# First loads and warm-up of a two-branch attention kernel: one weight quarter behind a small activation, warm-up matmuls on a constant

## Chip, cores and metric

The kernel runs on one core of one Trainium2 chip. The metric is the device time of one execution in microseconds, so smaller is better. Each figure is a median of several runs unless it is called a profile, which is one execution.

## The reference

```python
x = A_x                                             # (1, 2048, 1024), bf16
g = sigmoid((x * gate_w).sum(-1, keepdims=True))
a = _A_ref(x, A_wqkv, A_wo)                         # linear attention, 32 heads of 32
b = _B_ref(x, B_wqkv, B_wo)                         # dilated local window of 8 keys
return g * a + (1 - g) * b

def _A_ref(x, wqkv, wo):
    q, k, v = split(x @ wqkv)                       # cut: reshape to heads
    phi = lambda t: where(t > 0, t + 1, exp(t)) + 1e-6
    # cut: kv = phi(k)^T v, num = phi(q) kv, den = phi(q) . sum(phi(k)), o = num / den
    return o @ wo
```

Only the beginning matters here: the first work on TensorE is `x @ wqkv` for the keys of branch A. It needs x transposed and the key weights.

## The kernel before

The kernel loads x transposed (`xT`) and the key weights (`WkA`, two halves of 512 columns) in slices of the contraction dimension. A slice `k` holds two blocks of 128 rows; its 128x2x512 piece of one half is called a quarter here, because a half has four of them. The first quarters (k=0) of both halves go out on ScalarE's DMA queue. All other loads go out on SyncE's.

```python
nc.scalar.preload_act_table_set("natural_log_exp_and_others")
# ... cut ...
load_wk(nc.scalar, 0, 0)          # first half, first quarter
load_wk(nc.scalar, 0, 1)          # second half, first quarter
with tc.manual_schedule(engines={SP}):
    load_xT(0, 0, 2)              # "the first transpose": 256 rows of x, slice 0
    load_xT(0, 2, 4)              # "the second transpose"
    for k in range(1, 4):
        load_wk(nc.sync, k, 0)
        load_xT(k, 0, 4)
        load_wk(nc.sync, k, 1)
    # ... cut: the rest of x, other weights ...
```

While these loads are on their way, TensorE runs matmuls on a tile of ones. Their result is thrown away; they are there to bring its clock up early (it was up at 4.48 us in the profile of this kernel, with 34 of them).

```python
onesb = junk.tile([P, P], BF16, name="onesb")
nc.vector.memset(onesb[:], 1.0)
# ... cut ...
def warm_up(n):
    warm = ps_1.tile([P, P], F32, name="warm", tag="p1")
    for i in range(n):
        nc.tensor.matmul(warm[:], lhsT=onesb[:], rhs=onesb[:], start=True, stop=True)
warm_up(34)
# ... cut ...
for k in range(4):
    for half in range(2):
        for t in range(4):
            for kt in (2 * k, 2 * k + 1):
                project(first[4 * half + t], t, kt, half)     # 128x512 matmul, L168
            # ... cut: exp and the rest of phi when k == 3 ...
```

So the first four projections need the first transpose and the first quarter, the next four the second transpose, and the ninth needs the second half's first quarter.

The softmax here doesn't subtract the row's maximum and nothing guards it: scores larger than these inputs give would overflow.

## Time and profile before

| | before |
|---|---|
| median of 3 runs | 473.79 us (473.56 to 474.19) |
| span of the profile | 472.1 us |
| TensorE busy | 467.1 us, 99% |
| first warm-up matmul | 1.12 us |
| first transpose of x landed | 5.57 us |
| first projection | 5.62 us |

These are lines of the page of the profile before: the span, busy time by engine, the granted clock in 40 slices, the chain of waits by engine, and the group of the first projections (busy us and mean ns of one, then idle time before it and what ended it).

```profile
span 472.1 us, 13169 instructions
...
PE 467.1 (99%) x5762; PEld 244.3 (52%) x5762; DVE 277.8 (59%) x602; ACT 169.0 (36%) x272; POOL 15.4 (3%) x30
...
PEclk9999999999999999999999999999999999999999
...
PE 98%; DMA 1%; ACT 0%; issue 0%
...
L168 PE MATMUL pk_ps<-WkA,xT 128*128 128x512 bf16 x256 | 55.4, 379 | 0.8 <-DMA xT<-in_A_x_dram 0.8
```

TensorE bounds the kernel; the only other entry of size on the chain is 1% of DMA. The chain in order of time (start us, length us, what) shows where that DMA stands:

```profile
0.80 4.77 DMA xT<-in_A_x_dram
...
5.62 4.49 PE pk_ps L168 x20
```

The whole DMA part is the wait for the first transpose. The timeline of TensorE up to 9 us (start, length, engine, line, operation, count, then idle time before it in brackets) and of ScalarE with its DMA queue up to 6 us:

```profile
1.12 3.66 PE L174 MATMUL warm<-onesb 128*128 128x128 bf16 x34 [1.12 <-DVE onesb L165]
5.62 3.63 PE L168 MATMUL pk_ps<-WkA,xT 128*128 128x512 bf16 x16 [0.84 <-DMA xT<-in_A_x_dram]
```

```profile
0.80 1.28 ACT L68 ACT_TABLE_LOAD   x1 [0.80 <-PEq L627]
0.83 0.96 ACTq L98 DMA_DIRECT2D WkA<-in_A_wqkv_dram  x2
```

The warm-up begins once VectorE has filled the ones and ends 0.84 us before the first projection. Sixteen projections take 3.63 us. The two DMA issues of ScalarE's queue take place during the table load; the second one began at 1.31 us. TensorE waited for two things in the first 30 us (total, times, longest):

```profile
PE warm L174 <- DVE onesb L165: 1.1, 1, 1.1
PE pk_ps L168 <- DMA xT<-in_A_x_dram: 0.8, 1, 0.8
```

The trace also holds every DMA packet. The first quarter's 256 packets start between 1.9 and 3.3 us, the second's between 3.4 and 4.6 us. The first transpose's data packets start between 2.9 and 3.9 us, and its closing semaphore writes only at 4.4 to 4.6 us, when the second quarter is through.

### The profile page before, as it was taken

The numbers are of one execution on the slowest core, as the hardware profiler recorded it, in microseconds if no ns is written. First come the engines' busy times: TensorE is split into PE (matmuls) and PEld (weight loads), VectorE is DVE, ScalarE is ACT, GpSimd is POOL, SyncE is SP. The second block draws the span as 40 slices with busy tenths as digits, with TensorE's granted clock in tenths as the row PEclk, the third lists the DMA queues.
The fourth block names the chain that finished last, engine by engine and source line by source line (L and its number), as shares of the span: only waits on it lengthen the run. The fifth ranks groups of instructions, "written<-read, shape, count | busy, mean of one in ns | idle before, by whom it ended". The sixth has DMA issues, their size and how long they took to land.

```text
span 472.1 us, 13169 instructions
## 1 busy us (share of the span) xinstructions
PE 467.1 (99%) x5762; PEld 244.3 (52%) x5762; DVE 277.8 (59%) x602; ACT 169.0 (36%) x272; POOL 15.4 (3%) x30
## 2 busy tenths in 40 slices
PE   8999999999999999999999999999999999999997
PEld 5444444445444444445666666666664444444444
DVE  0586689990329999999566676767660049800000
ACT  1343321112443333333555555555551134221122
POOL 2300000500000000000000000000000000000000
PEclk9999999999999999999999999999999999999999
DMA  8999970000743233627327526452663923211111
GB/s 195 227 250 373 348 235 0 0 1 1 233 116 111 88 141 128 156 95 249 108 53 106 109 54 90 99 94 50 93 170 70 216 74 78 73 51 45 35 35 44
DMA packets 98781, 55.40 MB, mean 117 GB/s; under 512 B 70179, under 2 KB 90659, under 8 KB 98723
## 3 DMA queue, kind: packets, MB, share of 16 engines
q1 hardware_dynamic: 93282, 49.84, 41.5%
q10 hardware_dynamic: 5440, 4.72, 3.1%
q8 instruction: 45, 0.74, 0.7%
q14 instruction: 14, 0.11, 0.1%
HBM read 26.10 MB, written 15.86 MB: 89 GB/s over the span
## 4 chain that ended last, share of the span: by engine, by line
PE 98%; DMA 1%; ACT 0%; issue 0%
PE q_ps L387 27%; PE d_ps L584 12%; PE p_ps L294 12%; PE pk_ps L168 12%; PE g_ps L219 12%; PE e_ps L584 12%; PE p_ps L330 9%; PE po L466 2%; PE s2b L444 2%; DMA xT<-in_A_x_dram 1%; PE kv_ps L239 0%; PE w_ps L282 0%; ACT osb L589 0%
## 5 line engine op out<-in xcount | busy, mean ns | idle before, releaser
L387 PE MATMUL q_ps<-xT,WqB 64*64 64x512 bf16 x1024 | 68.3, 377 | 0.0
L387 PE MATMUL q_ps<-xT,WkB 64*64 64x512 bf16 x1024 | 67.9, 377 | 0.0
L153 DVE TENSOR_SCALAR e<-e 128x512 f32<-128x512 f32 x64 | 27.1, 423 | 62.9 <-ACT e L152 62.9
L294 PE MATMUL p_ps<-WvB,xT 128*128 128x512 bf16 x256 | 57.9, 379 | 0.0
L168 PE MATMUL pk_ps<-WkA,xT 128*128 128x512 bf16 x256 | 55.4, 379 | 0.8 <-DMA xT<-in_A_x_dram 0.8
L219 PE MATMUL g_ps<-pk,xrow 128*128 128x512 bf16 x256 | 55.4, 379 | 0.0
L449 ACT ACTIVATE PT<-s2b 128x928 bf16<-128x928 f32 (+4 forms) x40 | 34.2, 855 | 45.6 <-PE s2b L444 45.6
L451 DVE TENSOR_TENSOR PT<-PT,mask 128x928 bf16<-128x928 bf16 (+4 forms) x40 | 23.6, 590 | 37.8 <-ACT PT L449 37.8
L330 PE MATMUL p_ps<-WqA,xT 128*128 128x512 bf16 x192 | 43.4, 379 | 0.0
L584 PEld LDWEIGHTS <-pqT 128*128 128x128 bf16 x272 | 26.0, 98 | 29.7 <-issue 0.4
L584 PEld LDWEIGHTS <-OBT 128*128 128x128 bf16 x272 | 26.0, 98 | 29.4
L168 PEld LDWEIGHTS <-xT 128*128 128x128 bf16 x256 | 25.0, 98 | 31.0 <-DMA xT<-in_A_x_dram 1.0
L219 PEld LDWEIGHTS <-xrow 128*128 128x128 bf16 x256 | 25.0, 98 | 30.2
L294 PEld LDWEIGHTS <-xT 128*128 128x128 bf16 x256 | 24.6, 98 | 30.0 <-issue 0.9
L387 PEld LDWEIGHTS <-WkB 64*64 64x64 bf16 x1024 | 31.7, 107 | 15.4 <-issue 0.4
L387 PEld LDWEIGHTS <-WqB 64*64 64x64 bf16 x1024 | 31.5, 106 | 15.6 <-issue 0.9
L152 ACT ACTIVATE e<-pk_ps 128x512 f32<-128x512 f32 x32 | 18.9, 597 | 40.7 <-PE pk_ps L168 36.5
L299 ACT CAST tmp<-p_ps 128x512 bf16<-128x512 f32 x32 | 18.8, 590 | 37.3 <-PE p_ps L294 31.6
L584 PE MATMUL d_ps<-WoA,pqT 128*128 128x512 bf16 (+1 forms) x136 | 30.9, 370 | 0.0
L584 PE MATMUL d_ps<-WoB,OBT 128*128 128x512 bf16 (+1 forms) x136 | 30.8, 370 | 0.0
L330 PEld LDWEIGHTS <-xT 128*128 128x128 bf16 x192 | 18.8, 98 | 22.7
L584 PE MATMUL e_ps<-WoA,pqT 128*128 128x512 bf16 (+2 forms) x136 | 30.0, 363 | 0.0
(62 smaller groups left out, 484.2 us busy)
## 6 DMA issues: line engine op xcount, KB each, us to landing
vd<-tmp SPq DMA_DIRECT2D x16, 264.0 KB
xrow<-in_A_x_dram SPq DMA_DIRECT2D x4, 1024.0 KB
out_dram<-osb ACTq DMA_DIRECT2D x31, 128.0 KB
pqd<-tmp SPq DMA_DIRECT2D x12, 256.0 KB
WvA<-in_A_wqkv_dram SPq DMA_DIRECT2D x2, 1024.0 KB
WoA<-in_A_wo_dram SPq DMA_DIRECT2D x2, 1024.0 KB
WvB<-in_B_wqkv_dram SPq DMA_DIRECT2D x2, 1024.0 KB
WqA<-in_A_wqkv_dram SPq DMA_DIRECT2D x2, 1024.0 KB
```

The source lines that it names most:

```text
L152: nc.scalar.activation(out=e[:], in_=pj[:], func=ACT.Exp)
L153: nc.vector.tensor_scalar(out=e[:], in0=e[:], scalar1=1.0, scalar2=1e-6, op0=ALU.min, op1=ALU.add)
L168: nc.tensor.matmul(pj[:], lhsT=xT[:, kt, t * P:(t + 1) * P], rhs=WkA[half][:, kt, :], start=(kt == 0), stop=(kt == KT - 1))
L219: nc.tensor.matmul(pj[:], lhsT=xrow[:, t, kt * P:(kt + 1) * P], rhs=pk[:, t, half * 512:(half + 1) * 512], start=(t == 0), stop=(t == NB - 1))
L294: nc.tensor.matmul(st["pj"][:], lhsT=xT[:, kt, t * P:(t + 1) * P], rhs=WvB[half][:, kt, :], start=(kt == 0), stop=(kt == KT - 1))
L299: nc.scalar.copy(out=v[:, half * 16:(half + 1) * 16, 0:Dh], in_=st["pj"][:].rearrange("p (h e) -> p h e", h=16))
L330: nc.tensor.matmul(st["pj"][:], lhsT=xT[:, kt, t * P:(t + 1) * P], rhs=WqA[half][:, kt, :], start=(kt == 0), stop=(kt == KT - 1))
L387: nc.tensor.matmul(banks[o][64 * j:64 * j + 64, :], lhsT=lhsT(r, kt, j), rhs=rhs(r, kt), start=first and kt == 0, stop=kt == KT - 1, skip_ ...
L444: nc.tensor.matmul(s2b[64 * par:64 * par + 64, pair, :, o:o + w], lhsT=kts[c][r, par, k0:k0 + 64], rhs=qz[r, :, par, q0 % 512:q0 % 512 + w ...
L449: nc.scalar.activation(out=pt[:, :, 0:W_], in_=s2b[:].rearrange("p a b s -> p (a b) s")[:, :, 0:W_], func=ACT.Exp, scale=SCALE)
L451: nc.vector.tensor_tensor(out=pt[:, :, 0:W_], in0=pt[:, :, 0:W_], in1=mask[:, None, base:base + W_].broadcast_to([P, 4, W_]), op=ALU.mult)
L584: nc.tensor.matmul(st["ps"][:, 0:n], lhsT=lhsT, rhs=W[c0 // 512][:, c, c0 % 512:c0 % 512 + n], start=(side == 0 and c == 0), stop=(side == ...
```

## The change

The intent, as the edit reads: TensorE should not wait for VectorE's memset before it warms up, and the second half's first quarter should stay out of the way of the first transpose, since it is needed only for the ninth projection. The constant `ones` has one element per partition and is read with a step of 0. The trace has it filled at 0.37 us, before the first instruction of the kernel's body at 0.80 us, so nothing has to wait for it.

```diff
--- before.py
+++ after.py
@@ -99,9 +99,12 @@
                       in_=A_wqkv[2 * k * P:(2 * k + 2) * P, D + 512 * h:D + 512 * h + 512]
                       .rearrange("(kt p) n -> p kt n", p=P))
 
-    load_wk(nc.scalar, 0, 0)
-    load_wk(nc.scalar, 0, 1)
-    with tc.manual_schedule(engines={SP}):
+    ones = nc.const_aps.tensor(1.0, [P, P], BF16)
+    with tc.manual_schedule(engines={SP, mybir.EngineType.Activation}):
+        load_wk(nc.scalar, 0, 0)
+        first_act = consts.tile([P, 1], BF16, name="first_act")
+        nc.scalar.activation(out=first_act[:], in_=ones[:, 0:1], func=ACT.Exp)
+        load_wk(nc.scalar, 0, 1)
         load_xT(0, 0, 2)
         load_xT(0, 2, 4)
         for k in range(1, 4):
@@ -161,8 +164,6 @@
             work = s1.enter_context(tc.tile_pool(name="work1", bufs=3))
 
             s1.enter_context(tc.manual_schedule(engines={DVE}))
-            onesb = junk.tile([P, P], BF16, name="onesb")
-            nc.vector.memset(onesb[:], 1.0)
             pk = big.tile([P, NB, D], BF16, name="pk", tag="pkO")
             def project(pj, t, kt, half):
                 nc.tensor.matmul(pj[:], lhsT=xT[:, kt, t * P:(t + 1) * P], rhs=WkA[half][:, kt, :],
@@ -171,10 +172,10 @@
             def warm_up(n):
                 warm = ps_1.tile([P, P], F32, name="warm", tag="p1")
                 for i in range(n):
-                    nc.tensor.matmul(warm[:], lhsT=onesb[:], rhs=onesb[:], start=True, stop=True)
-
-
-            warm_up(34)
+                    nc.tensor.matmul(warm[:], lhsT=ones, rhs=ones, start=True, stop=True)
+
+
+            warm_up(37)
 
             def bank_k(i):
                 return (ps_1.tile([P, 512], F32, name="pk1_ps", tag="p1") if i & 4 else
```

In the compiled order of instructions only these things differ: one activation more on ScalarE between the two DMA issues, one memset less on VectorE, three warm-up matmuls more on TensorE.

## The prediction

> **What bounds the kernel now.** TensorE. The page gives PE 467.1 us of the 472.1 us span (99%); the chain of waits is 98% PE. Its one other part of size is at the start: 4.77 us (1%) until the first DMA transpose of x has landed. The timeline shows the first real projection at 5.62 us, after PE idled 0.8 us for that transpose; from there PE is almost never idle. So the change can gain only by landing that transpose earlier, at most about 0.8 us.
>
> **The start, from the records of single packets.** ScalarE's queue issues the two first weight quarters at 0.83 and 1.31 us. The first quarter's packets run 1.9 to 3.3 us, the second's 3.3 to 4.5 us. The first transpose's data packets run 2.9 to 3.9 us, and its closing semaphore writes come at 4.4 to 4.6 us, just when the second quarter is finished; it lands at 5.57 us. So the second quarter (256 packets of 1 KB, 46 ns each on 16 engines, about 0.74 us) stands between the transpose and its landing. It is not needed until eight matmuls (8 x 0.216 us) after the start.
>
> **What the change does.**
> 1. It puts a 128x1 activation between the two weight issues; the order of instructions shows nothing else moved. The activation runs behind the table load, which ends at 2.08 us. On ScalarE and VectorE this trace shows semaphore instructions 5 to 25 ns after the start of the instruction ahead, so I expect the second issue held to about 2.1 us (0.8 us later). The first issue's packets came 1.1 us after it; so the second quarter would start near 3.2 to 3.4 us, hardly later than now, because its packets already stand behind the first quarter's. That gains 0 to 0.3 us. [...]
> 2. Warm-up without the memset (0.17 us on VectorE): PE starts near 0.85 us instead of 1.12. Three more matmuls, 107 ns apart while cold, end it about where it ended (4.78 us). Before, the clock rose at 4.48 us, 3.36 us after the first warm-up[...]. I expect 4.2 us. Worth nothing itself, as PE then waits for x.
>
> Later loads have slack: the k=1 transpose lands at 7.96 us and is needed at 9.08.
>
> **Prediction.** 473.4 us, 8 in 10 within 472.7 to 474.2. Faster by over 2%: 0. Within 2%: 0.99. Slower by over 2%: 0.01.
>
> **What would show it.** Second weight issue at 2.1 us or later; first warm-up near 0.85 us; first projection at 5.0 to 5.6 us; everything after the same, only shifted.
>
> **What would make it wrong.** The sequencer issues the second DMA without waiting for the activation: no change. The constant has one element per partition, read with a step of 0: if TensorE reads that slower, the warm-up runs past 5.6 us and costs up to 3 us. The clock rises after the real matmuls began. The delayed quarter collides with the second transpose and the k=1 loads.

The sum came to 473.4 us, 0.4 us under the 473.79 us of the kernel before. The 4.2 us for the clock is the 0.85 us of the first warm-up plus the 3.36 us.

## The result

| | before | changed |
|---|---|---|
| median of 6 runs | 474.1 us (473.56 to 475.9) | 473.65 us (473.46 to 474.01) |
| span of the profile | 472.1 us | 472.3 us |
| first warm-up matmul | 1.12 us | 0.84 us |
| second issue on ScalarE's queue | 1.31 us | 1.35 us |
| first transpose landed | 5.57 us | 5.51 us |
| first projection | 5.62 us | 5.56 us |
| full clock from | 4.48 us | 6.40 us |

The ratio of the runs is 0.9987 with a 95% interval of 0.9971 to 1.0004: the same. One of the six runs of the kernel before, 475.9 us, is of the slow group explained below; without it the two means differ by 0.06% (an estimate from the single runs). The last row is the trace's record of TensorE's clock. The views do not show it (their clock line is what the throttle granted, 1.00 all along in both), but the spacing of matmuls does: in the profile before, the warm-up matmuls start 107 ns apart up to 4.40 us and the last two 56 ns apart (4.498 and 4.554 us).

The page of the changed kernel, the same lines:

```profile
span 472.3 us, 13144 instructions
...
PE 466.0 (99%) x5734; PEld 244.7 (52%) x5765; DVE 277.4 (59%) x601; ACT 169.1 (36%) x273; POOL 15.4 (3%) x30
...
PE 98%; DMA 1%; issue 0%; ACT 0%
...
L169 PE MATMUL pk_ps<-WkA,xT 128*128 128x512 bf16 x251 | 55.6, 381 | 0.9 <-DMA xT<-in_A_x_dram 0.6
```

A few matmul records are missing from this trace (251 of 256 projections), so its busy figure is slightly low. The chain has not changed. Timeline of TensorE and of ScalarE, and TensorE's waits, as above:

```profile
0.84 4.11 PE L175 MATMUL warm<-const-bfloat16-1.0 128*128 128x128 bf16 x37 [0.84 <-PEq L628]
5.56 3.81 PE L169 MATMUL pk_ps<-WkA,xT 128*128 128x512 bf16 x14 [0.61 <-DMA xT<-in_A_x_dram]
```

```profile
0.80 1.28 ACT L68 ACT_TABLE_LOAD   x1 [0.80 <-PEq L628]
0.83 0.96 ACTq L98 DMA_DIRECT2D WkA<-in_A_wqkv_dram  x2
2.09 0.20 ACT L106 ACTIVATE first_act<-const-bfloat16-1.0 128x1 bf16<-128x1 bf16 x1
```

```profile
PE warm L175 <- PEq L628: 0.8, 1, 0.8
PE pk_ps L169 <- DMA xT<-in_A_x_dram: 0.6, 1, 0.6
```

Two things stand out. The two DMA issues are still one piece of 0.96 us from 0.83 us on. The activation starts at 2.09 us, 0.3 us after the second issue is over: the quarter did not stay behind it. And the warm-up starts 0.28 us earlier and 0.06 us are won at the first projection, yet the profile's span is 0.2 us longer. The starts of the first four projections tell why: 5.615, 5.841, 6.057, 6.273 us before, and 5.557, 5.959, 6.386, 6.616 us after. Two steps of 0.40 and 0.43 us in place of 0.22 cost 0.40 us, as the clock rose only at 6.40 us. In that one execution the later clock ate more than the earlier start won: the net 0.34 us are still there at the first `g_ps` matmul (61.22 against 60.88 us) and 0.2 at the end; where the rest came back was not followed.

### The profile page after: what moved, and what is told of

Read it like the earlier page. It is cut to its first block, busy times and chain, and to the rows that moved or that the text cites. A ratio compares the mean times of both kernels' runs of the same rounds, so it can differ in the third digit from the quotient of the medians. Undisturbed runs are those within 1.5% of the kernel's fastest.

```text
span 472.3 us, 13144 instructions
## 1 busy us (share of the span) xinstructions
PE 466.0 (99%) x5734; PEld 244.7 (52%) x5765; DVE 277.4 (59%) x601; ACT 169.1 (36%) x273; POOL 15.4 (3%) x30
## 4 chain that ended last, share of the span: by engine, by line
PE 98%; DMA 1%; issue 0%; ACT 0%
PE q_ps L388 27%; PE d_ps L585 12%; PE pk_ps L169 12%; PE p_ps L295 12%; PE g_ps L220 12%; PE e_ps L585 11%; PE p_ps L331 9%; PE po L467 2%; PE s2b L445 2%; DMA xT<-in_A_x_dram 1%; PE kv_ps L240 0%; PE w_ps L283 0%; ACT osb L590 0%
## 5 line engine op out<-in xcount | busy, mean ns | idle before, releaser
L585 PE MATMUL e_ps<-WoB,OBT 128*128 128x512 bf16 (+2 forms) x133 | 29.7, 363 | 0.2
```

The source lines that it names most:

```text
L585: nc.tensor.matmul(st["ps"][:, 0:n], lhsT=lhsT, rhs=W[c0 // 512][:, c, c0 % 512:c0 % 512 + n], start=(side == 0 and c == 0), stop=(side == ...
```

## The experiments

The theory after the first look has three parts.

1. The activation holds nothing back: the DMA was issued at 1.35 us, while the activation still waited for the engine, which the table load kept until 2.08 us. So the loads are as before.
2. The second quarter does stand between the first transpose and its landing, and truly holding it would bring the landing forward.
3. The differences of 0.2 to 2 us between runs of one kernel come from the moment at which TensorE's clock rises. The idle time between warm-up and first projection has a part in that moment.

The third part starts from the two profiles. The clock rose 3.36 us after the first warm-up matmul in the profile before and 5.57 us after it in that of the changed kernel (at 4.48 and 6.40 us). So it does not rise at one fixed time after the warm-up begins. Once up it is recorded at full for 467.626 us in both, about the whole rest of the span. What does set the moment these traces do not show.

### act_only: only the activation between the two issues

```diff
+    ones = nc.const_aps.tensor(1.0, [P, P], BF16)
-    load_wk(nc.scalar, 0, 0)
-    load_wk(nc.scalar, 0, 1)
-    with tc.manual_schedule(engines={SP}):
+    with tc.manual_schedule(engines={SP, mybir.EngineType.Activation}):
+        load_wk(nc.scalar, 0, 0)
+        first_act = consts.tile([P, 1], BF16, name="first_act")
+        nc.scalar.activation(out=first_act[:], in_=ones[:, 0:1], func=ACT.Exp)
+        load_wk(nc.scalar, 0, 1)
```

> Only the activation between the two weight issues, warm-up as before (memset, 34 matmuls). Theory (the activation holds nothing back, because no wait connects it to the DMA): the second quarter is issued at 1.3 to 1.4 us, ahead of the activation at 2.09 us; the first transpose lands at 5.5 to 5.6 us; first projection at 5.55 to 5.65 us; time within 0.1% of before apart from when the clock rises. Rival (the queue is held, and the profile of the changed kernel was an exception): second issue at 2.1 us or later and the landing at least 0.2 us earlier.

Measured: median 473.71 us against 474.43 for the kernel before in the same rounds, ratio 0.9982 (0.9962 to 1.0002). The timeline of ScalarE in this run:

```profile
0.83 0.97 ACTq L98 DMA_DIRECT2D WkA<-in_A_wqkv_dram  x2
2.09 0.20 ACT L106 ACTIVATE first_act<-const-bfloat16-1.0 128x1 bf16<-128x1 bf16 x1
```

The second issue began at 1.34 us, the activation at 2.09: not held, as the theory says. The landing (5.28 us) and first projection (5.33 us) were earlier than the 5.5 to 5.65 us forecast. As the issue order in time was unchanged, this is the spread of one load between executions, not the activation: the four other profiles with this activation in this place landed it at 5.51 to 5.63 us, the three without it at 5.57 to 5.66. Four of the eleven runs of the kernel before in these rounds were of a slow group that is explained below. Without those four its mean is 474.07 us against 473.81 here, which is 0.05% (an estimate from the single runs).

### warm_only: only the constant and 37 matmuls

```diff
-            onesb = junk.tile([P, P], BF16, name="onesb")
-            nc.vector.memset(onesb[:], 1.0)
-                    nc.tensor.matmul(warm[:], lhsT=onesb[:], rhs=onesb[:], start=True, stop=True)
+                    nc.tensor.matmul(warm[:], lhsT=ones, rhs=ones, start=True, stop=True)
-            warm_up(34)
+            warm_up(37)
```

> Only the warm-up part: constant ones, no memset, 37 matmuls; weight issues as before. Theory [...]: warm-up from 0.84 us; [...]first projection at 5.55 to 5.65 us, its matmuls 0.43 us apart until the clock has risen; time within 0.1% of before. Rival (the step-0 constant warms the array less, so the clock always rises late): the clock rises after 6 us again, and a time 0.2 to 0.5 us longer than before.

Measured: median 474.04 us (473.46 to 475.72), ratio 0.9995 (0.9971 to 1.0019). Its profile fell on one of two runs at 475.7 us. TensorE up to 9 us:

```profile
0.84 4.11 PE L173 MATMUL warm<-const-bfloat16-1.0 128*128 128x128 bf16 x37 [0.84 <-PEq L626]
5.70 3.59 PE L167 MATMUL pk_ps<-WkA,xT 128*128 128x512 bf16 x8 [0.76 <-DMA xT<-in_A_x_dram]
```

Eight projections take the 3.59 us in which sixteen ran in the kernel before. The clock rose at 9.69 us, 8.85 us after the first warm-up matmul; the theory's range for it, which is cut, ended before that and was missed. From 5.70 to 9.69 us at half speed loses 2.0 us. The four runs outside that pair were between 473.46 and 474.11, 1.6 to 2.3 us shorter, so the clock does not always rise late with the constant (the second profile of the changed kernel, below, has it at 4.91 us); that rival falls.

The kernel before has the same two groups. Of its 38 runs beside the changed kernel and all these experiments, 8 were between 475.77 and 476.27 us and the other 30 at 474.81 or less. Runs of this upper kind, from 475.69 us on, are called the slow group below.

### held: the activation made a real wait

```diff
-        first_act = consts.tile([P, 1], BF16, name="first_act")
-        nc.scalar.activation(out=first_act[:], in_=ones[:, 0:1], func=ACT.Exp)
+        nc.scalar.activation(out=WkA[1][:, 0, 0:1], in_=ones[:, 0:1], func=ACT.Exp)
```

The element is overwritten by the load, so the result stays right and the DMA has to wait for the activation.

> The changed kernel, with the activation writing one element of the second quarter's tile, so that its DMA waits for the activation. Theory: second issue at about 2.35 us (activation ends 2.29), its packets from about 3.45 us, which is where they begin now; the first transpose lands at 5.3 to 5.6 us, so at most 0.2 us gained. Rival (the issue order is what matters): landing at 5.0 us or earlier, time 0.5 us shorter.

Measured: median 474.73 us (473.72 to 475.21), ratio 1.0 (0.9979 to 1.002). ScalarE and TensorE:

```profile
0.83 0.45 ACTq L98 DMA_DIRECT2D WkA<-in_A_wqkv_dram  x1
2.09 0.21 ACT L105 ACTIVATE WkA<-const-bfloat16-1.0 128x1 bf16<-128x1 bf16 x1
2.33 0.41 ACTq L98 DMA_DIRECT2D WkA<-in_A_wqkv_dram  x1
```

```profile
5.11 1.28 PE L168 MATMUL pk_ps<-WkA,xT 128*128 128x512 bf16 x4 [0.16 <-DMA xT<-in_A_x_dram]
8.00 4.27 PE L168 MATMUL pk_ps<-WkA,xT 128*128 128x512 bf16 x19 [1.61 <-DMA xT<-in_A_x_dram]
```

The issue moved to 2.33 us, and the first transpose landed at 5.06 us, earlier than the 5.3 to 5.6 us of the theory's arithmetic. But after four projections TensorE stood still for 1.61 us: the second transpose landed at 7.95 us in place of 5.94, and the quarter at 7.75 in place of 5.20. Both theories missed this. In the lines that follow stand the stretch (us), its length, busy time of PE, granted clock, DMA share and GB/s: of the kernel before in two stretches, then of this run, and then of `sp_quarter`, an experiment below in which nothing of ScalarE's queue stands beside the second transpose:

```profile
4.00:5.00 1.00, 0.77 (x9) 1.00 1.17 283
5.00:6.00 1.00, 0.39 (x2) 1.00 0.87 215
```

```profile
4.00:5.00 1.00, 0.94 (x9) 1.00 0.50 100
5.00:6.00 1.00, 0.90 (x3) 1.00 1.05 134
```

```profile
4.00:5.00 1.00, 1.00 (x10) 1.00 0.58 124
5.00:6.00 1.00, 1.00 (x5) 1.00 0.77 246
```

Between 4 and 6 us the DMA engines moved 100 and 134 GB/s where the kernel before moved 283 and 215. The 100 alone is no sign of trouble, as `sp_quarter` moved 124 there; the 134 is. The plainest measure is the second transpose itself: from the start of its first packet to that of its last took 2.92 us here, 1.00 in the kernel before and 1.31 in `sp_quarter`. The load that was held back had been issued and had not landed while the second transpose ran, and both crawled.

### held_long and held_long_again: a longer wait

```diff
-        nc.scalar.activation(out=WkA[1][:, 0, 0:1], in_=ones[:, 0:1], func=ACT.Exp)
+        nc.scalar.activation(out=WkA[1][:, 0:2, :], in_=nc.const_aps.tensor(1.0, [P, 2, 512], BF16), func=ACT.Exp)
```

> As the run before, but the activation writes all of the second quarter's tile (128x1024), about 1.04 us instead of 0.2. Theory (the second quarter's 256 packets stand between the first transpose's data and its closing writes): issue at about 3.2 us, packets from about 4.3 us, the first transpose's closing writes at about 4.0 us in place of 4.4, landing at 4.7 to 5.1 us, first projection at 4.9 to 5.1 us, the second quarter landed by 6.5 us, in time; time 0.4 to 0.7 us shorter (0.9985 to 0.999 of before). Rival (the transpose's closing writes wait for its own data alone, and come at 4.4 us for that): landing stays at 5.5 us and the time as before.

Measured: median 473.58 us (473.5 to 473.88), ratio 0.9979 (0.9958 to 1.0). ScalarE and TensorE:

```profile
0.83 0.45 ACTq L98 DMA_DIRECT2D WkA<-in_A_wqkv_dram  x1
2.09 1.05 ACT L105 ACTIVATE WkA<-const-bfloat16-1.0 128x1024 bf16<-128x1024 bf16 x1
3.17 0.39 ACTq L98 DMA_DIRECT2D WkA<-in_A_wqkv_dram  x1
```

```profile
4.80 1.97 PE L168 MATMUL pk_ps<-WkA,xT 128*128 128x512 bf16 x8 [0.19 <-DMA xT<-in_A_x_dram]
7.16 5.12 PE L168 MATMUL pk_ps<-WkA,xT 128*128 128x512 bf16 x23 [0.40 <-DMA WkA<-in_A_wqkv_dram]
```

The first transpose's closing writes came at 3.3 to 3.6 us, it landed at 4.75 us and the projections began at 4.80 us, 0.8 us earlier than before. Part 2 of the theory holds. In the kernel before, the last of the transpose's own data packets started at 3.91 us and the closing writes only from 4.43 us on, with the second quarter's packets in between. Here the last data packet started at 3.55 us and the closing writes were through at 3.61. The data itself was 0.36 us earlier; the rest of the gain is the closing writes. The traces show the order, not its reason. But the quarter itself landed at 7.12 us, and the ninth projection, which would have started 0.22 us after the eighth at 6.38 us, started at 7.16: 0.56 us of the gain were given back there (the view's 0.40 counts from a modelled end). In the same stretches as above:

```profile
4.00:5.00 1.00, 0.81 (x10) 1.00 0.64 122
5.00:6.00 1.00, 1.00 (x6) 1.00 1.03 239
```

These are close to the 124 and 246 of `sp_quarter`: the second transpose was hindered little, with 1.62 us from first to last packet. The landing forecast for the quarter, 6.5 us, was missed, and at the first `g_ps` matmul 0.2 us of the 0.8 are left (60.68 against 60.88 us). The ratio of 0.9979 flatters the run: against the mean of 474.07 us without the slow group the gain is 0.09%, again an estimate. The repeat on another chip:

> The run with the long activation once more, on this chip beside the others: first projection at 4.7 to 5.0 us, about 0.5 to 0.8 us of it given back in waits for the second quarter (landing near 7.1 us); times 473.4 to 473.9, none above 474.3.

Measured: median 473.62 us (473.49 to 474.07), ratio 0.9984 (0.9964 to 1.0004); first projection at 4.74 us, although the first transpose had landed at 4.45: the 37 warm-up matmuls were in the way until then. The quarter landed at 6.68 us, and not it but the k=1 part of x, landed at 9.00 us in place of 7.96, held TensorE up (0.4 us).

### held_mid: half the wait

```diff
-        nc.scalar.activation(out=WkA[1][:, 0:2, :], in_=nc.const_aps.tensor(1.0, [P, 2, 512], BF16), func=ACT.Exp)
+        nc.scalar.activation(out=WkA[1][:, 0, :], in_=nc.const_aps.tensor(1.0, [P, 512], BF16), func=ACT.Exp)
```

> As the long activation, but half as wide (128x512, about 0.63 us): issue near 2.77 us, between the run with one element (2.33 us; second transpose landed only at 7.95 us) and the long one (3.18 us; 5.68 us). If the trouble of the one-element run is the second transpose and the quarter being in flight together, this run has it too, in part: first transpose landed at 4.7 to 5.1 us, second transpose landed between 5.7 and 8 us, the quarter at 7 to 8 us, TensorE idle 0.5 to 2 us before the ninth projection. If it was chance, both land by 6.6 us and nothing idles.

Measured: median 474.96 us of 4 runs (474.38 to 476.48), ratio 1.0016 (0.999 to 1.0041). Issue at 2.75 us; first transpose landed at 5.02, second at 7.57, quarter at 7.35 us; TensorE waited 1.2 us before the fifth projection. One run, 476.48 us, shows a mean granted clock of 0.996 where the others show 1.0; it was not profiled. So `held` was no chance. The second transpose took longer from first to last packet the earlier the quarter had been issued: 2.92 us in `held` (issue at 2.33), 2.33 here (2.75), 1.62 and 1.38 in the two profiles of the long wait (3.18), each from one profile. That the packets get in each other's way is not shown: here 170 packets of the second transpose started between 3.75 and 4.5 us, against 410 in `sp_quarter`, and the quarter's first packet started only at 4.46. Between 5 and 6 us the DMA engines moved 150 GB/s here, against 134 in `held` and 246 in `sp_quarter`. Why a quarter that is issued but not yet moving goes with a slow transpose, these runs do not tell.

### sp_quarter: the quarter behind both transposes on SyncE's queue

```diff
-        first_act = consts.tile([P, 1], BF16, name="first_act")
-        nc.scalar.activation(out=first_act[:], in_=ones[:, 0:1], func=ACT.Exp)
-        load_wk(nc.scalar, 0, 1)
         load_xT(0, 0, 2)
         load_xT(0, 2, 4)
+        load_wk(nc.sync, 0, 1)
```

> The changed kernel without the activation, the second half's first quarter issued on SyncE's queue after the two first transposes. Theory: with nothing of ScalarE's queue beside them the first transpose lands at 4.7 to 5.1 us as in the run with the long activation, the quarter starts behind the second transpose (packets from about 4.9 us) and lands at 6.3 to 6.7 us, about when it is needed (6.5 us); the k=1 loads come 0.6 us later and may cost up to 0.3 us; the first g_ps matmul at 60.3 to 60.7 us; six runs at 473.2 to 473.7, none slow, since the gap after the warm-up is gone. Rival (the quarter only moves its cost to the next load): stall of 0.8 us later, time as the changed kernel's 473.7.

Measured: median 473.99 us (473.72 to 474.4), ratio 0.9991 (0.9972 to 1.0009). The first transpose landed at 4.54 us and the projections began at 4.74, when the warm-up was over. The quarter landed at 6.97 us, 0.3 us later than the latest forecast, and the first k=1 weights and x at 7.96 and 9.36 us in place of 7.04 and 7.96. TensorE then waited 0.2 us for weights and 0.5 us for x (the lines below), and the first `g_ps` matmul came at 61.22 us, after the 60.88 of the kernel before. The rival was right: the wait only moved to the next loads.

```profile
PE pk_ps L167 <- DMA xT<-in_A_x_dram: 0.5, 1, 0.5
PE pk_ps L167 <- DMA WkA<-in_A_wqkv_dram: 0.2, 1, 0.2
```

### warm45, warm20 and before42: the idle time after the warm-up

The three kernels change one number: 45 and 20 in place of 37 in the changed kernel, 42 in place of 34 in the kernel before.

```diff
-            warm_up(37)
+            warm_up(45)   # warm20: warm_up(20)
```

```diff
-            warm_up(34)
+            warm_up(42)   # before42, all else as before
```

> The changed kernel with 45 warm-up matmuls in place of 37, so that while cold (107 ns each) they last until 5.64 us and leave TensorE no idle time before the first projection. Theory [...]: [...]no run above 474.5 us, all six between 473.4 and 474.3. Rival (the slow runs come from the chip or from DMA, not from the warm-up's gap): some of its runs at 475.5 to 476.3 as the kernel before has.

> The changed kernel with 20 warm-up matmuls in place of 37: they end at 2.97 us, and the idle time before the first projection is 2.6 us. Theory: [...]most of its six runs at 474.9 to 476.6, median near 475.7. Rival (20 warm-up matmuls are enough, or it is their number and not their timing): as the changed kernel, near 473.7.

> The kernel before with 42 warm-up matmuls in place of 34 and nothing else: cold, they last from 1.12 to 5.60 us. Theory: the group of its slow runs (475.7 to 476.3, 5 of its 14 runs so far) is gone; all six runs between 473.4 and 474.4, median near 473.8; mean 0.1 to 0.2% under that of the kernel before. Rival (what the changed kernel gained is the constant or the weight issue): slow runs as before.

(17 runs of the kernel before up to then, 5 of them slow.)

Measured in the same rounds: warm45 474.02 us (473.91 to 474.23, 5 runs), warm20 476.11 us (475.12 to 477.09, 5 runs), before42 473.95 us (473.89 to 474.94, 5 runs); the kernel before 474.19 us (473.73 to 476.24, 10 runs). The ratios are 1.0 (0.9986 to 1.0013), 1.0045 (1.0031 to 1.0058) and 1.0002 (0.999 to 1.0015). TensorE in warm45 up to 9 us and in warm20 up to 12 us:

```profile
0.84 4.96 PE L175 MATMUL warm<-const-bfloat16-1.0 128*128 128x128 bf16 x45 [0.84 <-PEq L628]
5.63 3.61 PE L169 MATMUL pk_ps<-WkA,xT 128*128 128x512 bf16 x14
```

```profile
0.84 2.29 PE L175 MATMUL warm<-const-bfloat16-1.0 128*128 128x128 bf16 x20 [0.84 <-PEq L628]
5.67 6.57 PE L169 MATMUL pk_ps<-WkA,xT 128*128 128x512 bf16 x16 [2.54 <-DMA xT<-in_A_x_dram]
```

With 45 matmuls the first projection follows the warm-up with no idle time shown; the clock rose at 6.07 us, and no run is in the slow group. With 20 the idle time is 2.54 us, the clock rose at 11.66 us, a little after the latest time forecast for it (cut with its rule), and sixteen projections took 6.57 us in place of 3.6. All five of its runs are 0.9 us or more above the kernel before's median. One run of before42 at 474.94 us misses the forecast's 474.4; it is not in the slow group. The 0.1 to 0.2% forecast for before42 was not met either; in these rounds only one of the ten runs of the kernel before was in the slow group, so there was little to win.

The clock's rise in all thirteen profiles, beside the idle time that the timeline shows before the first projection:

| profile | idle before the first projection | clock rose at |
|---|---|---|
| before | 0.84 us | 4.48 us |
| changed | 0.61 us | 6.40 us |
| warm_only | 0.76 us | 9.69 us |
| warm20 | 2.54 us | 11.66 us |
| the nine others | 0.19 us or less in the four whose timeline was asked for (held, held_long, held_long_again, warm45) | 4.09 to 6.07 us |

The longest idle time goes with the latest rise, but 0.84, 0.61 and 0.76 us go with 4.48, 6.40 and 9.69 us: the idle time alone does not give the moment. Counted from the end of the last warm-up matmul's stream (by the spacing of the matmuls) the kernel before, the changed one and warm_only have 0.8 to 1.0 us up to the first projection (the profile's own idle times of 0.61 to 0.84 us count from a modelled end, which is later). What a late rise costs the spans show: the span less the start of the first projection and less half of the projection time before the clock's rise is 466.3 to 466.5 us in seven of the eight profiles without a stall among the first projections (466.8 in before42), although these spans differ by 3.1 us.

### after_again: the changed kernel once more

> The changed kernel once more, unaltered, for the spread of its runs. Theory: its warm-up leaves a gap of about 0.77 us cold (before: 0.87)[...]: 0 to 2 of its six runs at 475.3 to 476, the others 473.4 to 474.2; before on the same chip 1 run in 3 slow. Second weight issue at 1.35 us again. Rival (the change removes the slow runs): none of the six above 474.3.

Measured: median 473.78 us (473.71 to 474.36, 5 runs), ratio 0.9997 (0.9984 to 1.0009). Second issue at 1.34 us, activation at 2.09, first transpose landed at 5.61 us, first projection at 5.65 us, clock up at 4.91 us. None of its runs is in the slow group, which both readings allowed.

Taken together, none of the changed kernel's 11 runs was in the slow group, against 8 of the 38 of the kernel before, but 2 of 6 of warm_only, which has the changed kernel's warm-up, and none of 6 of act_only, which has the warm-up of before. Whether the change makes slow runs rarer is therefore left open. That the idle time does is shown at the end of its range (warm20, five of five at 475.12 us or more, the one profiled with a late clock) and supported at the other: none of 28 runs of the kernels with 0.4 us or less between warm-up and first projection and no long stall after it (warm45, before42, held_long twice, sp_quarter), against 10 of 61 of those with 0.8 to 1.0 us. `held` and `held_mid`, which stall for more than 1 us after the first four projections, are in neither count, and the runs are of different chips and rounds.

## Why the prediction was right or wrong

- **What bounds the kernel: right.** TensorE is busy 99% before and after, the first transpose is the only wait of size, and the time stayed within the range (473.65 us in 472.7 to 474.2; predicted 473.4). That the change "can gain only by landing that transpose earlier" leaves out the clock, whose late rise cost 2.0 us in the profile of warm_only.
- **"I expect the second issue held to about 2.1 us": wrong, and this is the step that failed.** It was issued at 1.35 us, 0.74 us before the activation. The prediction read the hold from semaphore instructions that follow the start of the instruction ahead by 5 to 25 ns. Those stood behind instructions that themselves wait for semaphores (all 91 on ScalarE and all 41 on VectorE that follow within 60 ns in the profile before); whether that sets their timing was not tested. It was carried over to an activation that waits for none and a DMA that does not depend on it. act_only and the second profile of the changed kernel show the same, with the issue at 1.34 us in both and the activation at 2.09. The list of what would make the prediction wrong named this case, with "no change" as its effect, and that is what came.
- **"Hardly later than now", a gain of 0 to 0.3 us if held to 2.1 us: wrong in both directions.** `held`, issued at 2.33 us, landed the first transpose 0.5 us earlier, and lost 1.61 us on the second one. The arithmetic took the packets' start from one duration and left out that the second transpose would slow down, to 2.92 us from first to last packet in place of 1.00.
- **The second quarter stands between the first transpose and its landing: right.** held_long and sp_quarter landed it at 4.45 to 4.75 us. The prediction stopped at the landing, though: later waits took back most of those 0.8 us. The slack that it gave the k=1 transpose (landed at 7.96, needed at 9.08 us) was gone once the loads had moved: 9.36 us in sp_quarter, 9.00 in held_long_again.
- **A pause after the table load: none here.** The activation began 11 ns after the load ended (2.089 and 2.078 us).
- **Warm-up from 0.85 us: right (0.84). The clock at 4.2 us: wrong.** It was 6.40 us in one profile of the changed kernel and 4.91 in another. The prediction added the 3.36 us of the profile before to the first warm-up matmul; in these two the rise came 5.57 and 4.07 us after it. It did list a late clock among its risks. Nor is the warm-up "worth nothing itself": its end decides how long TensorE idles before the first projection, and with 2.54 us of idle time (warm20) the clock rose at 11.66 us and all five runs took 475.12 us or more.
- **The step-0 constant read more slowly: did not occur.** Warm-up matmuls are 107 ns apart in both kernels.

In short: the forecast time was right because the gain it reckoned with was small, not because the queue was held. As to the mechanism that is luck.

## What to carry to other kernels

Program order on an engine's queue was not a hold here: the activation delayed the later DMA only where a wait connected the two (issue at 2.33 us in `held`, at 1.34 and 1.35 us without a wait), so look for the wait in the compiled order and for the issue time in the trace. Bringing the first load forward helped here only as far as the loads right behind it kept up (`held`: 0.5 us won, 1.61 us of waiting right after); check the next two before counting the gain, and check what is in flight together. Let the warm-up matmuls reach close to the first real one: with an idle gap of 0.8 to 1.0 us here one run in six (10 of 61) was about 2 us longer, with 0.4 us or less none of 28, and a profile of one execution cannot tell such a kernel from its neighbour. Of the versions tried, the one with the long activation had the lowest medians (473.58 and 473.62 us), but its ratio to the kernel before is still called the same.
